# Fused linear attention and softplus FFN on one core: another order of the first x, conversions ahead of softplus in tile 0, joined weights side by side

## The chip, the cores and the metric

The kernel runs on one core of a Trainium2 chip. The metric is the time of one execution in device microseconds; a kernel's time is the median of its runs. The engines are named as in the profile: PE is TensorE (PEld its weight loads), DVE VectorE, ACT ScalarE, POOL GpSimd, SP the queue of SyncE that issues the DMAs.

## What is computed

Attention without a score matrix, and behind it a feed-forward layer whose activation is softplus. There are 8 batches, 8 heads, 576 tokens a batch and 64 elements a head, so 4608 tokens of 512 elements for the layer, whose inner width is 2048.

```python
q_s = np.exp(q - np.max(q, axis=-1, keepdims=True))
q_s = q_s / (np.sum(q_s, axis=-1, keepdims=True) + 1e-09)
k_s = np.exp(k - np.max(k, axis=2, keepdims=True))
k_s = k_s / (np.sum(k_s, axis=2, keepdims=True) + 1e-09)
kv = np.einsum('bhsd,bhse->bhde', k_s, v)
x = np.einsum('bhsd,bhde->bhse', q_s, kv)        # then (4608, 512)
h = x @ w_in                                     # (4608, 2048)
g = np.maximum(h, 0.0) + np.log1p(np.exp(-np.abs(h)))
return g @ w_out
```

## The kernel before

The tokens go in 9 tiles of 512, the inner width in 16 blocks `j` of 128. A step is one pair (tile, j). The loop over steps gives out, in this order: `up` (the product of x with a block of w_in, into one of the two PSUM banks `ph`), the share of the next tile's attention that stands in this step's slots, the end of the last step's softplus, this step's `softplus`, and `down` of two steps before (the product of g with a block of w_out, into four banks `po`). Each engine works through its instructions in the order in which the code gives them out; waits between engines follow from the data.

Tile 0 is computed in full float32: four matmuls for `up` and four for `down` (each shown as two records). Later tiles use three products of a high and a low part (float32r) in place of each. Weights arrive as int64 words `w` and are converted during tile 0: `top_w` (L119, ScalarE), `scale_w` (L114, ScalarE), `sign_w` (L124, VectorE, or GpSimd for the first three) and `join_w` (L135, VectorE) leave a float32 for each int64, in every other word. `split_w` (L142) makes the high part on ScalarE and the low part on VectorE; the list `SPLITS` has the steps in which the 16 blocks are split, and a block must be split before tile 1 comes to it.

`attend(t + 1)` spreads the attention of the next tile over the 16 steps of a tile. For the k and v of a pair of heads (a unit `h`) there are six parts: `top` (VectorE, the maximum over chunks, `mx`, L184, whose transposition L186 stands on TensorE at the end of the step), `across` (the maximum over the transposed tile, L200, and its transposition L201), `shift` (L205, subtraction on VectorE), `product` (the exponential L211 on ScalarE, and the k-v products L216 on TensorE at the end of the step), `scale` (L226, L227: r) and `split` (L240 `kv_hi` on ScalarE, L243 `kv_lo` on VectorE). Units h and h + 2 share a PSUM bank `att` and one of two buffers of k and v. When the products of unit h are given out, the DMA of the unit after next is issued (L169, the bulk, and L172, its tail). The slots of tile 1 and tile 2 are `2*h + i` for i in (0, 1, 2, 3, 4, 4). `q_unit` has 12 parts for the softmax of q, and `x_unit` makes x of q and kv (`q_lo`, L330, and the products L337 to L339).

Softplus (L387) has four ScalarE rows (L395 to L398) and three VectorE rows: L399 `(w - 1) - u`, L400 `max(ph, 0) - w`, which is the last reader of the PSUM bank `ph`, and L401. In tile 0 the conversions of w(j+2) are given out behind softplus(j).

The start, up to the first `up`, follows an order written by hand: a string of names, of which "u" are kv units, "q" the softmax of q, "x" the first x (transpose, product, copy for each pair of heads), and "t m s j" the conversions of the first weights.

## Time and profile before

| | |
|---|---|
| time, median of 3 runs | 921.27 us (919.81 to 922.92) |
| profiled execution | 920.85 us, span 919.1 us, granted clock 0.991 |
| PE busy | 883.2 us (96%) |
| DVE busy | 700.7 us (76%) |
| ACT busy | 582.7 us (63%) |
| POOL busy | 67.0 us (7%) |

The span is the time from the first to the last instruction of the profiled execution; 1.75 us of the execution lie outside it. Busy is the time in which an engine had an instruction under way. A row of the timeline has the start, the duration, the engine, the line, the operation, the tile written and those read, their shapes and, in brackets, how long the engine was idle before and which instruction ended that wait.

### The profile page before, as it was taken

To read this page: it belongs to the slowest core of one execution; us is meant where nothing else is said; L and a number is where in the kernel's file an instruction comes from. 1 tells how busy PE (TensorE), PEld (TensorE's weight loads), DVE (VectorE), ACT (ScalarE), POOL (GpSimd) and SP (SyncE) were. 2 spreads that over 40 slices of the span, in tenths; PEclk is the share of its full clock that TensorE was granted. 3 is DMA by queue.
4 is the path that set the end of the run, shared out by engine and by line. 5 is a ranking of instruction groups with operands and counts; after the bars stand their busy time and mean duration, and the time that the engine had idled before them with its cause. 6 is when DMAs were issued, how large, how long until landed. Compare 5 with 4: busy or idle time off the path is not lost.

```text
span 919.1 us, 11673 instructions
## 1 busy us (share of the span) xinstructions
PE 883.2 (96%) x4196; PEld 680.2 (74%) x4196; DVE 700.7 (76%) x1094; ACT 582.7 (63%) x982; POOL 67.0 (7%) x119
## 2 busy tenths in 40 slices
PE   3799989989999999999999999999999999999998
PEld 2343444667788888888888888888888888888886
DVE  8798878788778877887688768976897676765553
ACT  4666566767656665666576657665675566656554
POOL 2302300000000100020002000100110000000000
PEclk9899989999999999999999999999999999999999
DMA  9945101111013101301130113011200110001001
GB/s 313 381 141 195 52 0 47 46 53 32 21 46 98 36 17 47 98 23 30 46 98 9 44 46 98 1 52 46 84 16 1 46 47 1 1 1 47 0 1 46
DMA packets 49034, 55.28 MB, mean 60 GB/s; under 512 B 2256, under 2 KB 39120, under 8 KB 47824
## 3 DMA queue, kind: packets, MB, share of 16 engines
q1 hardware_dynamic: 48400, 54.27, 17.9%
q8 instruction: 33, 0.54, 0.2%
q10 hardware_dynamic: 576, 0.26, 0.1%
q14 instruction: 25, 0.20, 0.1%
HBM read 45.09 MB, written 9.44 MB: 59 GB/s over the span
## 4 chain that ended last, share of the span: by engine, by line
PE 83%; DVE 8%; ACT 5%; issue 2%; DMA 1%; POOL 0%; SPq 0%; DVEq 0%; ACTq 0%; POOLq 0%
PE ph L382 12%; PE po L427 12%; PE po L429 12%; PE po L428 12%; PE ph L383 12%; PE ph L384 12%; PE ph L377 3%; PE po L423 3%; PE att L216 2%; DVE w L138 1%; DVE w L128 1%; PE att L339 1%; PE att L338 1%; PE att L337 1%; DMA kvt<-in_kv_tail 1%
## 5 line engine op out<-in xcount | busy, mean ns | idle before, releaser
L429 PE MATMUL po<-w,g_lo 128*128 128x512 f32 x480 | 187.2, 390 | 1.9 <-DVE g_lo L407 1.9
L382 PE MATMUL ph<-x,w 128*128 128x512 f32 x480 | 188.8, 393 | 0.0
L427 PE MATMUL po<-w,g_hi 128*128 128x512 f32 x480 | 187.6, 391 | 0.0
L383 PE MATMUL ph<-x,w 128*128 128x512 f32 x480 | 186.9, 389 | 0.0
L428 PE MATMUL po<-w,g_hi 128*128 128x512 f32 x480 | 186.9, 389 | 0.0
L384 PE MATMUL ph<-x,w 128*128 128x512 f32 x480 | 186.8, 389 | 0.0
L399 DVE SCALAR_TENSOR_TENSOR w<-w,u 128x512 f32<-128x512 f32 x134 | 92.5, 690 | 117.1 <-ACT w L397 116.9
L406 ACT CAST g_hi<-l 128x512 fp32r<-128x512 f32 x128 | 79.5, 621 | 137.1 <-DVE l L401 134.9
L395 ACT ACTIVATE u<-ph 128x512 f32<-128x512 f32 x134 | 80.2, 598 | 55.6 <-PE ph L384 50.7
L401 DVE SCALAR_TENSOR_TENSOR l<-l,ln,w 128x512 f32<-128x512 f32 x128 | 96.3, 752 | 14.6
L429 PEld LDWEIGHTS po<-w,g_lo 128*128 128x128 f32 x480 | 90.1, 188 | 21.7 <-DVE g_lo L407 2.7
L382 PEld LDWEIGHTS ph<-x,w 128*128 128x128 f32 x480 | 90.4, 188 | 19.7 <-issue 0.6
L384 PEld LDWEIGHTS ph<-x,w 128*128 128x128 f32 x480 | 90.1, 188 | 19.0
L427 PEld LDWEIGHTS po<-w,g_hi 128*128 128x128 f32 x480 | 90.2, 188 | 18.0
L383 PEld LDWEIGHTS ph<-x,w 128*128 128x128 f32 x480 | 90.2, 188 | 17.9
L428 PEld LDWEIGHTS po<-w,g_hi 128*128 128x128 f32 x480 | 90.1, 188 | 17.8
L407 DVE TENSOR_TENSOR g_lo<-l,g_hi 128x512 fp32r<-128x512 f32 x128 | 87.1, 680 | 15.5 <-ACT g_hi L406 14.1
L400 DVE SCALAR_TENSOR_TENSOR w<-ph,w 128x512 f32<-128x512 f32 x134 | 92.6, 691 | 4.6
L397 ACT ACTIVATE w<-u 128x512 f32<-128x512 f32 x134 | 84.8, 633 | 4.2
L396 ACT ACTIVATE u<-u 128x512 f32<-128x512 f32 x134 | 84.7, 632 | 4.3
L398 ACT ACTIVATE l<-u 128x512 f32<-128x512 f32 x128 | 79.2, 619 | 12.5 <-DVE g_lo L407 12.5
L377 PE MATMUL ph<-x,w 128*128 128x512 f32 x128 | 61.6, 627 | 0.0
(136 smaller groups left out, 1020.7 us busy)
## 6 DMA issues: line engine op xcount, KB each, us to landing
kvt<-in_kv SPq DMA_DIRECT2D x30, 512.0 KB, 4.8
qt<-in_q SPq DMA_DIRECT2D x9, 1024.0 KB, 4.8
w<-in_w_in SPq DMA_DIRECT2D x16, 512.0 KB, 8.1
w<-in_w_out SPq DMA_DIRECT2D x16, 512.0 KB, 8.9
out<-w SPq DMA_DIRECT2D x32, 256.0 KB, 2.3
kvt<-in_kv_tail SPq DMA_DIRECT2D x28, 64.0 KB, 4.5
x<-in_kv SPq DMA_DIRECT2D x2, 512.0 KB, 9.4
out<-x SPq DMA_DIRECT2D x4, 256.0 KB, 2.4
```

The costliest lines, as they stand in the source:

```text
L377: nc.tensor.matmul(ph, lhsT=y[:, h * P:(h + 1) * P], rhs=x0[:, h], start=h == 0, stop=h == HP - 1)
L382: nc.tensor.matmul(ph, lhsT=w_hi, rhs=x_hi, start=h == 0, stop=False)
L383: nc.tensor.matmul(ph, lhsT=w_lo, rhs=x_hi, start=False, stop=False)
L384: nc.tensor.matmul(ph, lhsT=w_hi, rhs=x_lo, start=False, stop=h == HP - 1)
L397: nc.scalar.activation(w, u, AF.Copy, bias=1.0)
L399: nc.vector.scalar_tensor_tensor(out=w, in0=w, scalar=1.0, in1=u, op0=ALU.subtract, op1=ALU.subtract)
L400: nc.vector.scalar_tensor_tensor(out=w, in0=ph, scalar=0.0, in1=w, op0=ALU.max, op1=ALU.subtract)
L401: nc.vector.scalar_tensor_tensor(out=l, in0=l, scalar=ln1, in1=w, op0=ALU.subtract, op1=ALU.add)
L407: nc.vector.tensor_tensor(out=g_lo, in0=l, in1=g_hi.bitcast(F32), op=ALU.subtract)
L427: nc.tensor.matmul(po, lhsT=g_hi[:, ms], rhs=w_hi, start=j == 0, stop=False)
L428: nc.tensor.matmul(po, lhsT=g_hi[:, ms], rhs=w_lo, start=False, stop=False)
L429: nc.tensor.matmul(po, lhsT=g_lo[:, ms], rhs=w_hi, start=False, stop=j == NJ - 1)
```

## The change

The joined float32 weights now lie in the first half of their place, one next to the other (`whole_w`), and `up`, `down` and `split_w` of tile 0 read them there. The order of the start is another: `up` of step 0 is given out product by product (`up0` to `up3`), two of them between the first x products; the swap of q's sums goes by halves (`q12`, `q13`), both of q's divisions are on VectorE, and three of four x copies on ScalarE. In tile 0 the conversions of w(j+2) stand ahead of softplus(j), and the last two VectorE rows of softplus (`rest`) move behind the attention work of the next step. Eight blocks are split in tile 0 instead of six. For tiles 1 and 2 `top` of a kv unit stands directly behind the join, and `shift` goes to the step of `product`; tile 2's slots of q change by a step.

```diff
--- before.py
+++ after.py
@@ -37,7 +37,7 @@
 START = [P * sum(SUBS[:t]) for t in range(len(SUBS) + 1)]
 NTILE = len(SUBS)
 
-SPLITS = [10, 11, 12, 13, 14, 15, 16, 17, 18, 19, 20, 21, 22, 23, 24, 25]
+SPLITS = [6, 7, 8, 9, 10, 11, 12, 13, 16, 17, 18, 19, 21, 23, 25, 27]
 TOK = P * max(SUBS)
 assert START[-1] == NT
 
@@ -102,6 +102,9 @@
         w = raw[k].bitcast(dtype).rearrange("p z (n two) -> p (z n) two", two=2)
         return w[:, :, 0], w[:, :, 1]
 
+    def whole_w(k, dtype):
+        return raw[k].bitcast(dtype).rearrange("p z n -> p (z n)")[:, 0:2 * DM]
+
     def halves(k, dtype):
 
         w = raw[k].bitcast(dtype).rearrange("p z (n e) -> p (z n) e", e=4)
@@ -136,12 +139,12 @@
 
         low, high = words(k, U32)
         nc.vector.scalar_tensor_tensor(
-            out=low, in0=high, scalar=3, in1=low, op0=ALU.logical_shift_left, op1=ALU.bitwise_or
+            out=whole_w(k, U32), in0=high, scalar=3, in1=low, op0=ALU.logical_shift_left, op1=ALU.bitwise_or
         )
 
     def split_w(k):
 
-        y, _ = words(k, F32)
+        y = whole_w(k, F32)
         parts[k] = wp.tile([P, 2, 2, DM], F32R, name=f"w{k - 1}" if k else "spare")
         hi, lo = (parts[k][:, i].rearrange("p z n -> p (z n)") for i in range(2))
         nc.scalar.copy(hi, y)
@@ -281,9 +284,9 @@
 
         copy = nc.vector.tensor_copy if t else nc.scalar.copy
         if t:
-            slow = [nc.gpsimd if t == 1 else nc.vector] * 2
+            slow = [nc.gpsimd if t == 1 else nc.vector] * 4
         else:
-            slow = [nc.vector, nc.gpsimd]
+            slow = [nc.vector, nc.gpsimd, nc.vector, nc.vector]
 
         def join():
             nc.vector.tensor_tensor(out=m, in0=m, in1=swapped(m, copy), op=ALU.max)
@@ -297,18 +300,30 @@
         def total(g):
             nc.vector.tensor_reduce(out=s[:, g * n:(g + 1) * n], in_=half[g], op=ALU.add, axis=AX.X)
 
+        other = []
+
+        def swap(g):
+
+            if not other:
+                other.append(sm.tile([P, TOK // 8], F32, name="other"))
+            for a in range(4):
+                z = a ^ 1
+                copy(other[0][32 * a:32 * a + 32, g], s[32 * z:32 * z + 32, g])
+
         def invert():
-            o = swapped(s, copy)
+            if not other:
+                swap(slice(0, 2 * n))
+            o = other[0]
             nc.vector.scalar_tensor_tensor(out=s, in0=s, scalar=EPS, in1=o, op0=ALU.add, op1=ALU.add)
             nc.vector.reciprocal(s, s)
 
         def divide(g):
-            slow[g].tensor_tensor(out=half[g], in0=half[g], in1=spread(s, g), op=ALU.mult)
+            slow[2 + g].tensor_tensor(out=half[g], in0=half[g], in1=spread(s, g), op=ALU.mult)
 
         return [
             lambda: top(0), lambda: top(1), join, lambda: shift(0), lambda: shift(1),
             lambda: power(0), lambda: power(1), lambda: total(0), lambda: total(1), invert, lambda: divide(0), lambda: divide(1),
-        ]
+        ] + [lambda g=g: swap(slice(g * n, (g + 1) * n)) for g in range(2) if not t]
 
     def x_part(t, h):
 
@@ -361,7 +376,7 @@
             nc.tensor.matmul(bank, lhsT=whole[:, h], rhs=qT[:, h], start=True, stop=True)
 
         def take():
-            if h % 2 == 0:
+            if h < HP - 1:
                 nc.scalar.copy(x0[:, h], bank)
             else:
                 nc.vector.tensor_copy(x0[:, h], bank)
@@ -369,13 +384,22 @@
         return [flip, product, take]
 
 
+    begun = {}
+
+    def up_whole(j, h):
+
+        if h == 0:
+            begun[j] = ps_h.tile([P, TOK], F32, name="ph")
+        y = whole_w(j, F32)
+        nc.tensor.matmul(begun[j], lhsT=y[:, h * P:(h + 1) * P], rhs=x0[:, h], start=h == 0, stop=h == HP - 1)
+
     def up(t, j):
+        if t == 0:
+            if j not in begun:
+                for h in range(HP):
+                    up_whole(j, h)
+            return begun.pop(j)
         ph = ps_h.tile([P, TOK], F32, name="ph")
-        if t == 0:
-            y, _ = words(j, F32)
-            for h in range(HP):
-                nc.tensor.matmul(ph, lhsT=y[:, h * P:(h + 1) * P], rhs=x0[:, h], start=h == 0, stop=h == HP - 1)
-            return ph
         for h in range(HP):
             w_hi, w_lo = (parts[j][:, i, 0, h * P:(h + 1) * P] for i in range(2))
             x_hi, x_lo = (x_part(t, h)[:, i] for i in range(2))
@@ -388,7 +412,7 @@
 
         if t == 0:
 
-            u, w = (tp.tile([P, TOK], F32, name=("u", "w", "l")[(2 * j + i) % 3]) for i in range(2))
+            u, w = (tp.tile([P, TOK], F32, name=name) for name in ("u", ("w", "l")[j % 2]))
             l = gp.tile([P, TOK], F32, name=("g_hi", "g_lo")[j % 2])
         else:
             u, w, l = (tp.tile([P, TOK], F32, name=name) for name in ("u", "w", "l"))
@@ -397,9 +421,13 @@
         nc.scalar.activation(w, u, AF.Copy, bias=1.0)
         nc.scalar.activation(l, u, AF.Ln, bias=1.0)
         nc.vector.scalar_tensor_tensor(out=w, in0=w, scalar=1.0, in1=u, op0=ALU.subtract, op1=ALU.subtract)
-        nc.vector.scalar_tensor_tensor(out=w, in0=ph, scalar=0.0, in1=w, op0=ALU.max, op1=ALU.subtract)
-        nc.vector.scalar_tensor_tensor(out=l, in0=l, scalar=ln1, in1=w, op0=ALU.subtract, op1=ALU.add)
-        return l
+
+        def rest():
+            nc.vector.scalar_tensor_tensor(out=w, in0=ph, scalar=0.0, in1=w, op0=ALU.max, op1=ALU.subtract)
+            nc.vector.scalar_tensor_tensor(out=l, in0=l, scalar=ln1, in1=w, op0=ALU.subtract, op1=ALU.add)
+            return l
+
+        return rest
 
     def split_g(l):
         g_hi, g_lo = (gp.tile([P, TOK], F32R, name=name) for name in ("g_hi", "g_lo"))
@@ -416,7 +444,7 @@
             g_hi, g_lo = g
             w_hi, w_lo = (parts[j][:, i, 1] for i in range(2))
         else:
-            y, _ = words(j, F32)
+            y = whole_w(j, F32)
         for m, po in enumerate(acc[t]):
             ms = slice(m * P, (m + 1) * P)
             if t == 0:
@@ -489,13 +517,14 @@
 
         warm = ps_h.tile([P, TOK], F32, name="ph")
         todo["warm"] = lambda: [nc.tensor.matmul(warm[:, 0:P], lhsT=ident, rhs=ident, start=True, stop=True) for _ in range(8)]
+        todo.update({f"up{h}": lambda h=h: up_whole(0, h) for h in range(HP)})
         todo["kv"] = kv_prefetch
         todo["w"] = lambda: [load_w(k) for k in range(5, 10)]
         todo["q"] = lambda: q_load(1)
         for name in (
-            "q0 q1 u00 q2 q3 q4 q5 u10 u01 u11 u02 u12 q6 u03 u13 u20 u30 u21 u31 u22 u32 t0 m0 s0 u23 u33 warm q7 q8 q9 "
-            "kv kv w u04 u14 u05 u15 q10 q11 x00 x10 x01 x11 t1 m1 u24 u34 u25 u35 x20 x30 x21 x31 s1 j0 x02 x12 x22 x32 "
-            "t2 m2 s2 j1 q"
+            "q0 q1 u00 q2 q3 q4 q5 u10 u01 u11 u02 u12 q6 u03 u13 u20 u30 q7 u21 u31 t0 m0 s0 q8 q12 q13 u22 u32 u23 u33 "
+            "warm kv kv w q9 u04 u14 u05 u15 q10 t1 x00 x10 x01 x11 x02 m1 s1 x12 q11 j0 u24 u34 u25 u35 up0 up1 "
+            "x20 x30 x21 x31 x22 x32 up2 up3 j1 t2 m2 s2 q"
         ).split():
             todo[name]()
 
@@ -521,13 +550,19 @@
             if t < B:
                 for h in range(HP):
                     if t <= ON_PE:
-                        slots = [2 * h + i for i in (0, 1, 2, 3, 4, 4)]
+                        slots = [(first, 2 * h)] + [2 * h + i for i in (1, 3, 3, 4, 4)]
                     else:
 
                         g, z = 5 * (h // 2), h % 2
                         slots = [g + i for i in (z, z + 1, z + 1, 3, 4, 4)]
                     lazy(lambda h=h: kv_unit(t, h, banks[h % 2], after=kv_next), slots)
-            lazy(lambda: q_unit(t), (3, 4, 5, 5, 6, 7, 8, 7, 8, 9, 9, 10) if t == 1 else (2, 3, 3, 4, 5, 6, 6, 7, 8, 8, 9, 10))
+            if t == 1:
+                slots = 3, 4, 5, 5, 6, 7, 8, 7, 8, 9, 9, 10
+            elif t <= ON_PE:
+                slots = 1, 2, 3, 4, 5, 5, 6, 6, 7, 8, 9, 10
+            else:
+                slots = 2, 3, 3, 4, 5, 6, 6, 7, 8, 8, 9, 10
+            lazy(lambda: q_unit(t), slots)
             for h in range(HP):
                 a = h + 11
                 lazy(
@@ -560,13 +595,15 @@
                     for fn in steps[NJ]:
                         fn()
             if soft:
-                pending.append((soft[0], split_g(soft[1]) if soft[0][0] else soft[1]))
+                pending.append((soft[0], split_g(soft[1]) if soft[0][0] else soft[1]()))
                 soft = None
             if slot:
-                soft = slot, softplus(t, j, ph)
+
                 if t == 0 and 2 < j + 2 < NJ:
                     for fn in (top_w, scale_w, sign_w):
                         fn(j + 2)
+                l = softplus(t, j, ph)
+                soft = slot, l() if t else l
                 for fn in last[j]:
                     fn()
             while pending and order.index(pending[0][0]) <= n - 2:
```

VectorE's order in tile 0, step 4: before, from the sign step and the join of w(5) to the end of softplus(4) (L128 sign, L138 join, `kv_lo` and `mx` are the kv units 0 and 2).

```order
L128 TENSOR_SCALAR w_302<-w_302 128x1024
L138 SCALAR_TENSOR_TENSOR w_302<-w_302 128x1024
L226 TENSOR_SCALAR r<-att_105 128x1
L227 RECIPROCAL r<-r 128x1
L243 SCALAR_TENSOR_TENSOR kv_lo_101<-att_105,r,kv_hi_93 64x64 x2
L205 TENSOR_TENSOR kvt<-kvt,att_106 128x10x64
L184 TENSOR_REDUCE mx<-kvt 128x128
L280 TENSOR_REDUCE m<-qt 128x32
L252 TENSOR_TENSOR kv_lo_100<-spare,kv_hi_92 128x128
L399 SCALAR_TENSOR_TENSOR u<-u,l 128x512
L400 SCALAR_TENSOR_TENSOR u<-ph,u 128x512
L401 SCALAR_TENSOR_TENSOR g_hi<-g_hi,ln_109,u 128x512
```

The same place of the changed program: L131 is the sign step, L423 the first row of softplus(3), L141 the join, L187 `mx`, L246 `kv_lo`, L426 and L427 the deferred rows of softplus(3).

```order
L131 TENSOR_SCALAR w_304<-w_304 128x1024
L423 SCALAR_TENSOR_TENSOR l<-l,u 128x512
L141 SCALAR_TENSOR_TENSOR w_304<-w_304 128x1024
L187 TENSOR_REDUCE mx<-kvt 128x128
L229 TENSOR_SCALAR r<-att_105 128x1
L230 RECIPROCAL r<-r 128x1
L246 SCALAR_TENSOR_TENSOR kv_lo_101<-att_105,r,kv_hi_93 64x64 x2
L283 TENSOR_REDUCE m<-qt 128x32
L255 TENSOR_TENSOR kv_lo_100<-spare,kv_hi_92 128x128
L426 SCALAR_TENSOR_TENSOR l<-ph,l 128x512
L427 SCALAR_TENSOR_TENSOR g_lo<-g_lo,ln_109,l 128x512
```

The maximum `mx` stands ahead of r and `kv_lo` instead of behind them and `shift`, and the row that reads `ph` stands behind all of the attention work of the next step.

VectorE's order in tile 1, step 4, before: from the last row of softplus to `g_lo`.

```order
L401 SCALAR_TENSOR_TENSOR l<-l,ln_109,w 128x512
L226 TENSOR_SCALAR r<-att_105 128x1
L227 RECIPROCAL r<-r 128x1
L243 SCALAR_TENSOR_TENSOR kv_lo_97<-att_105,r,kv_hi_89 64x64 x2
L205 TENSOR_TENSOR kvt<-kvt,att_106 128x10x64
L184 TENSOR_REDUCE mx<-kvt 128x128
L292 TENSOR_TENSOR qt<-qt,m 128x1024
L148 TENSOR_TENSOR w_1188<-w_483,w_1188 128x1024
L407 TENSOR_TENSOR g_lo<-l,g_hi 128x512
```

The same place of the changed program.

```order
L427 SCALAR_TENSOR_TENSOR l<-l,ln_109,w 128x512
L187 TENSOR_REDUCE mx<-kvt 128x128
L229 TENSOR_SCALAR r<-att_105 128x1
L230 RECIPROCAL r<-r 128x1
L246 SCALAR_TENSOR_TENSOR kv_lo_97<-att_105,r,kv_hi_89 64x64 x2
L295 TENSOR_TENSOR qt<-qt,m 128x1024
L435 TENSOR_TENSOR g_lo<-l,g_hi 128x512
```

Here too `mx` comes before r and `kv_lo`; `shift` (L205) and the split of a block (L148) no longer stand in this step.

TensorE's order at the start, before: warm-up products, the four x products (L361), `up` of step 0 (L377), the transposition of tile 1's first `mx`, and `up` of step 1.

```order
L491 MATMUL ph<-ident 128x128 x8
L361 MATMUL po_179<-w_160,spare 128x512
L361 MATMUL po_180<-w_160,spare 128x512
L361 MATMUL po_181<-w_160,spare 128x512
L361 MATMUL po_182<-w_160,spare 128x512
L377 MATMUL ph<-x_161,w_142 128x512 x4
L186 MATMUL att_105<-ident,mx 128x128
L377 MATMUL ph<-x_161,w_145 128x512 x4
```

The same place of the changed program (L376 x products, L394 `up`).

```order
L519 MATMUL ph<-ident 128x128 x8
L376 MATMUL po_179<-w_160,spare 128x512
L376 MATMUL po_180<-w_160,spare 128x512
L394 MATMUL ph<-x_161,w_142 128x512 x2
L376 MATMUL po_181<-w_160,spare 128x512
L376 MATMUL po_182<-w_160,spare 128x512
L394 MATMUL ph<-x_161,w_142 128x512 x2
L189 MATMUL att_105<-ident,mx 128x128
L394 MATMUL ph<-x_161,w_145 128x512 x4
```

Two products of `up` now stand between the second and the third x product.

## Rows read from the trace of the kernel before

**Rows 1.** The page, the chain that ended last: shares of the span by engine

```profile
PE 83%; DVE 8%; ACT 5%; issue 2%; DMA 1%; POOL 0%; SPq 0%; DVEq 0%; ACTq 0%; POOLq 0%
```

**Rows 2.** Stages: start, end, length, busy us of PE, PEld, DVE, ACT, POOL, then PEclk

```profile
33.40:161.00 127.60, 119.23 (x354) 54.15 (x352) 107.18 (x141) 85.70 (x125) 16.79 (x17) 0.96 0.33 119
161.00:259.00 98.00, 92.19 (x460) 71.31 (x459) 80.82 (x126) 65.87 (x108) 1.94 (x12) 1.00 0.14 44
259.00:900.00 641.00, 641.00 (x3211) 532.18 (x3210) 478.38 (x755) 405.89 (x705) 37.76 (x74) 1.00 0.12 37
```

**Rows 3.** Timeline of TensorE around the first x and step 1 of tile 0

```profile
28.27 5.31 PE L361 MATMUL po<-w,spare 128*128 128x512 f32 x8 [2.90 <-DVE w L358]
33.41 3.60 PE L377 MATMUL ph<-x,w 128*128 128x512 f32 x8
...
42.68 0.32 PE L201 MATMUL att<-ident,m 128*128 128x128 f32 x1 [2.12 <-DVE m L200]
```

**Rows 4.** Timeline of TensorE around its two long waits in tile 0

```profile
82.51 0.33 PE L186 MATMUL att<-ident,mx 128*128 128x128 f32 x1 [2.09 <-DVE mx L184]
82.67 5.30 PE L377 MATMUL ph<-x,w 128*128 128x512 f32 x8
...
124.21 0.42 PE L337 MATMUL att<-q_hi,kv_hi 128*128 128x64 f32 x1 [2.57 <-DVE q_lo L330]
...
126.14 5.36 PE L377 MATMUL ph<-x,w 128*128 128x512 f32 x7
```

**Rows 5.** Waits of VectorE for softplus, 46 to 161 us

```profile
DVE u L399 <- ACT u L397: 2.8, 3, 1.5
```

**Rows 6.** VectorE operations by form, 46 to 161 us

```profile
L138 DVE SCALAR_TENSOR_TENSOR w<-w 128x1024 uint32<-128x1024 uint32 x13 | 18.9, 1457 | 0.4
L128 DVE TENSOR_SCALAR w<-w 128x1024 uint8<-128x1024 uint8 x13 | 17.2, 1326 | 2.0 <-ACT w L117 1.9
L148 DVE TENSOR_TENSOR w<-w,w 128x1024 fp32r<-128x1024 f32 x5 | 6.1, 1223 | 1.3 <-ACT w L147 1.3
```

**Rows 7.** Timeline of all engines at step 4 of tile 0

```profile
58.62 0.67 SPq L172 DMA_DIRECT2D kvt<-in_kv_tail  x1
...
59.70 1.23 DVE L138 SCALAR_TENSOR_TENSOR w<-w 128x1024 uint32<-128x1024 uint32 x1
...
60.84 0.15 DVE L226 TENSOR_SCALAR r<-att 128x1 f32<-128x1 f32 x1
...
61.47 3.77 PE L423 MATMUL po<-w,g_hi 128*128 128x512 f32 x8
...
61.95 0.58 DVE L243 SCALAR_TENSOR_TENSOR kv_lo<-att,r,kv_hi 64x64 fp32r<-64x64 f32 x2 [0.76 <-ACT kv_hi L240]
...
62.56 0.82 DVE L205 TENSOR_TENSOR kvt<-kvt,att 128x640 f32<-128x640 f32 x1
...
63.30 1.30 DVE L184 TENSOR_REDUCE mx<-kvt 128x128 f32<-128x640 f32 x1
...
64.52 1.21 DVE L280 TENSOR_REDUCE m<-qt 128x32 f32<-128x1024 f32 x1
...
66.56 0.69 DVE L400 SCALAR_TENSOR_TENSOR u<-ph,u 128x512 f32<-128x512 f32 x1
66.70 0.73 ACT L211 ACTIVATE kvt<-kvt 128x640 f32<-128x640 f32 x1
```

**Rows 8.** DMA view of tile kvt, 50 to 75 us, fastest, median, slowest landing

```profile
DMA to landing us min/median/max: 3.8/3.9/4.1
```

**Rows 9.** Timeline at step 4 of tile 1, and one wait of a later step

```profile
189.52 0.58 DVE L243 SCALAR_TENSOR_TENSOR kv_lo<-att,r,kv_hi 64x64 fp32r<-64x64 f32 x2 [0.76 <-ACT kv_hi L240]
...
191.39 1.32 DVE L184 TENSOR_REDUCE mx<-kvt 128x128 f32<-128x640 f32 x1 [0.43 <-DMA kvt<-in_kv_tail]
...
192.76 0.33 PE L186 MATMUL att<-ident,mx 128*128 128x128 f32 x1 [0.76 <-DVE mx L184]
...
224.09 0.50 PE L429 MATMUL po<-w,g_lo 128*128 128x512 f32 x1 [1.88 <-DVE g_lo L407]
```

## The prediction

> **What bounds the kernel now.** I read the chain of work that ended last, then the table of stages, then the waits one by one. The chain says where the end of the program is decided: 83% of it is TensorE, 8% VectorE and 5% ScalarE [rows 1]. So a microsecond counts only where TensorE stands still or runs slowly, and the table of stages says where that is [rows 2]. From 259 us to 900 us TensorE is busy for all of 641.00 us; nothing in the diff alters its instructions there, and the softplus and attention work of that stretch lies beside it. What the change can move lies before 259 us: the start (0 to 33.4 us), tile 0 in full float32 (33.4 to 161 us, TensorE 119.23 of 127.60 us busy, VectorE 107.18) and the first part of tile 1 (161 to 259 us, 92.19 of 98.00). In tile 0 TensorE is idle for 8.4 us only, and VectorE, which does the sign step and the join of the weights, has 20.4 us free. Neither has much room, so each wait of one is nearly a wait of both.
>
> The waits of TensorE there have names. At the start it waits 2.90 us for the transposed q ahead of the first x products, and 2.12 us in step 1 for the second maximum of k [rows 3]. In tile 0 it waits 2.09 us at 82.51 for a column maximum `mx` and 2.57 us at 124.21 for a `q_lo`. Behind both stands an `up` at half speed: 8 records in 5.30 us where the usual is 3.60, and 7 in 5.36 where 7/8 of 3.60 is 3.15 [rows 3, 4]. So each of these two places costs more than its wait: 2.09 + 1.70 = 3.8 us and 2.57 + 2.21 = 4.8 us. The granted clock of the stretch is 0.96 [rows 2].
>
> **The change, part by part.** The sum is made against the profiled execution, 920.85 us (span 919.1), which is 0.42 us under the median of 921.27.
>
> 1. The order of the first x. The first two `up` products of step 0 now stand between x products 1 and 2, q's division leaves GpSimd, and the swap of sums goes by halves on ScalarE. At best both waits go: 2.90 + 2.12 = -5.0 us. At worst they are only moved, 0: step 0 still needs the join `j0` and all of `s1`, and in step 0 the column maximum of tile 1's first unit now stands behind the join. I take -2.0, under half, because what TensorE waits for is VectorE work, and the start has as much of that as before.
>
> 2. Weights side by side. `down` of tile 0 streams the joined weights; it takes 3.77 us for 8 records where `up`, which streams the contiguous x0, takes 3.60 [rows 3, 7]. If the stride is the reason, 16 steps x 0.17 = -2.7 us at best; if VectorE sets the pace, 0. I take -1.0. The Trainium skill, SBUF — State Buffer (section on the ports, the note on cachelines), says that accesses which hit the same 16-byte line at least twice run at full bandwidth, so that a stride of two float32 words costs nothing; the trace shows 0.17 us a step that this rule doesn't explain, and by the rule the term would be 0 and the sum 1 us higher. The join and the split themselves read and write as many elements as before: 1.22 us for the split, and the join's 1457 ns (with its collisions) stay [rows 6].
>
> 3. Conversions ahead of softplus. ScalarE now does the two conversions of w(j+2) before softplus(j), and VectorE puts `sign` and `join` between the first row of softplus and its rest. What it takes away: VectorE's waits for ScalarE, of which the rows show 1.9 us ahead of `sign` and 2.8 us in three waits of the `u` form of softplus [rows 5, 6]. For TensorE that is worth at most what the late `q_lo` costs, 4.8 us, and at least 0. I take -3.0, nearer to the upper end, since `q_lo` is late there only because VectorE is.
>
> 4. The attention slots of tile 1 and 2, in tile 0. `top` of a kv unit moves from behind `kv_lo` and `shift` to right behind the join. But its k arrives by DMA. In step 4 the tail's DMA is issued at 58.62 and takes 3.8 us at least, so it lands at 62.4 [rows 7, 8]. The join ends at 60.93, so VectorE, which goes in order, would stand for 1.5 us there; before it did r, `kv_lo` and `shift` in that time. What is queued behind it: mx 1.30, to 63.7; r and `kv_lo`, 1.69 from 60.84 to 62.53 in the rows, to 65.4; q's maximum 1.21, to 66.6; and only then the row `max(ph,0)-w` (L400 before, L426 after; 0.69), to 67.3. That row frees the PSUM bank that the next `up` writes, and in the changed kernel it is deferred behind all of this. TensorE is through with `down` at 61.47 + 3.77 = 65.24. So it waits some 2.1 to 2.4 us (by 0.28 for the little split of `whole`): +2.2, between 0, if the DMA lands earlier, and +3.9 with an `up` at half speed behind it (1.70 more). In step 6 the same place already costs 2.09 us; there I put +0.2. The idle VectorE, twice 1.5 us, and the wait for the exponential of k, which now directly follows `shift` in the same step (0.82 + 0.73, [rows 7]), make VectorE late by up to 4.5 us in a stretch where it has little room: +2.0, between 0 and +4.5.
>
> 5. The splits. Eight instead of six stand in tile 0, from step 6 on: two more of 1.22 us and a wait of some 0.3 us each [rows 6] are 3.0 us of VectorE: +1.5, between 0 and +3.0.
>
> 6. Tile 1. There VectorE already waits 0.43 us for the tail's DMA ahead of mx, and TensorE 0.76 us for mx [rows 9]: the DMA is what ends last. After the change r and `kv_lo` come behind that mx. The next transposed maximum writes the bank that `kv_lo` reads, so it waits for another 1.69 us; two such units are +3.4. `shift` and exponential in one step put up to 1.55 us on the products of each unit; I take one of them, +1.5. The split beside the late `g_lo` goes away, and with it that wait of 1.88: -1.9 [rows 9]. Together +3.0, between -1.9 and +6.5.
>
> Sum: -2.0 - 1.0 - 3.0 + 2.2 + 0.2 + 2.0 + 1.5 + 3.0 = +2.9. From 920.85 this is 923.75, and with the 0.42 us to the median 924.2; I forecast 924.2 us. What can be told from no change here is about 0.3%, 2.8 us; the forecast lies 2.9 us above, at that edge.
>
> **The rivals.**
>
> Faster: VectorE gains its lead. If conversions ahead of softplus give VectorE enough lead that it reaches mx late, after the k has landed, its wait for the DMA is paid out of waits that go away anyway. Then the four named places in the start and tile 0 vanish: 5.0 + 3.8 + 4.8 = 13.6 us, less the two splits (3.0) and tile 1's 3.0: -7.6, about 914 us; with half of the places gone -1 to -3. For it: VectorE has 20.4 us free in tile 0, and a part of that is its waits for ScalarE. Against it: the landing is tied to the products of the step before (TensorE's work), not to VectorE, so a VectorE that is earlier only waits longer. It decides if mx shows no DMA wait in steps 4 and 6. Chance 0.27.
>
> No change: the start's gain (-2 to -5) and the attention slots' loss cancel; 919 to 923 us. Chance 0.23.
>
> Slower by the clock: each of the new waits of about 2 us (steps 4 and 6, and one or two in steps 8 to 10) is followed by an `up` at half speed, as the two were at 82.51 and 124.21. Three such steps more are 3 x 1.70 = 5.1 us: 929 us. Against it: the waits of tile 1 have no such step behind them; the granted clock is 1.00 in that stretch, against 0.96 in tile 0 [rows 2]. The Trainium skill, TensorE: Matmul & The Clock Gate (HAM oscillation), describes a kernel in which every wait for a DMA sends the array to half its clock; the two places here agree with it, the waits of tile 1 do not. Chance 0.14.
>
> My own case, slower by 1 to 7 us: 0.36.
>
> **How the numbers follow.** The likeliest case gives 924.2 us, with its own range of 921 to 928. The range for 8 in 10 reaches to the middle of the faster case and over the clock's: 912 to 931. Faster by over 0.3% has the faster case and a little of no change's lower end, 0.27; within 0.3%, no change and the lower part of my own case, 0.27; slower, the rest of my own case and the clock's, 0.46.
>
> **What would show it.** In the changed trace: the first x products without their 2.90 us; `down` of tile 0 at 3.60 us for 8 records (part 2); no wait of `sign` and of the first softplus row for ScalarE (part 3); a wait of mx for the k tail's DMA right behind the join in steps 4 and 6 of tile 0, and behind it TensorE waiting for the row `max(ph,0)-w` (part 4); in tile 1 the transposed maximum waiting for `kv_lo`, 1.5 us longer each (part 6). If tile 1's first `up` starts before 158 us instead of near 161, the faster rival is right. The prediction is wrong if the DMA lands before the join ends, or if TensorE's two slow `up`s disappear and none take their place.

## The result, and the profile after

The changed kernel takes 925.43 us (median of 8 runs, 922.78 to 927.95), the kernel before 921.53 us (8 runs). The ratio is 1.0038, with a 95% interval of 1.0025 to 1.005: slower by 3.5 us by the ratio, by 3.9 us by the medians. The profiled execution is the fastest of the 8 (922.78 us, span 921.0 us against 919.1), so its rows show some 2 us of the loss and not all of it.

The page of the changed kernel, busy times:

```profile
PE 879.6 (96%) x4196; PEld 678.8 (74%) x4196; DVE 699.3 (76%) x1094; ACT 582.2 (63%) x987; POOL 64.6 (7%) x118
```

TensorE is busy for less time than before (879.6 against 883.2 us) in a longer span. The table of stages, with the columns of [rows 2]:

```profile
33.40:161.00 127.60, 115.86 (x355) 53.20 (x355) 109.35 (x144) 86.78 (x127) 15.88 (x17) 0.97 0.33 119
161.00:259.00 98.00, 89.33 (x444) 69.48 (x443) 75.93 (x121) 60.72 (x103) 1.88 (x12) 0.98 0.12 37
259.00:900.00 641.00, 641.00 (x3210) 532.15 (x3209) 478.26 (x753) 406.99 (x708) 37.70 (x74) 1.00 0.12 38
```

From 33.4 to 161 us TensorE goes through as many records as before (355 against 354) in 3.4 us less busy time (115.86 against 119.23), most of which the faster `down` makes (16 steps of 0.17 us). From 161 to 259 us it does less work than before (444 records against 460, 89.33 us against 92.19), and the granted clock there is 0.98 instead of 1.00. From 259 us to 900 us nothing has changed. A fixed stretch holds other work in each kernel, though, so the timeline has to say where it went. TensorE's timeline of the start, to be read against [rows 3]:

```profile
26.71 1.88 PE L376 MATMUL po<-w,spare 128*128 128x512 f32 x4
...
35.89 0.33 PE L189 MATMUL att<-ident,mx 128*128 128x128 f32 x1 [1.22 <-DVE mx L187]
...
39.83 3.67 PE L394 MATMUL ph<-x,w 128*128 128x512 f32 x8
43.34 3.60 PE L451 MATMUL po<-w,g_hi 128*128 128x512 f32 x8
```

The x products come at 26.71 instead of 28.27 and at full speed (1.88 us for 4 records, where 8 took 5.31), `up` of step 1 at 36.06, behind a wait of 1.22 us for mx, and step 2's at 39.83, where before TensorE waited until 42.68 for a maximum. By `up` of step 3, 46.88, the changed kernel is 3.1 us ahead. `down` has 3.60 us for its 8 records, as `up`. Now step 4 of tile 0, the issue of the k tail, VectorE and then TensorE, the place of [rows 7]:

```profile
55.42 0.66 SPq L175 DMA_DIRECT2D kvt<-in_kv_tail  x1
55.50 1.22 DVE L141 SCALAR_TENSOR_TENSOR w<-w 128x1024 uint32<-128x1024 uint32 x1
59.45 1.28 DVE L187 TENSOR_REDUCE mx<-kvt 128x128 f32<-128x640 f32 x1 [2.73 <-DMA kvt<-in_kv_tail]
...
61.75 0.58 DVE L246 SCALAR_TENSOR_TENSOR kv_lo<-att,r,kv_hi 64x64 fp32r<-64x64 f32 x2 [0.76 <-ACT kv_hi L243]
...
63.79 0.69 DVE L426 SCALAR_TENSOR_TENSOR l<-ph,l 128x512 f32<-128x512 f32 x1
...
62.38 0.33 PE L189 MATMUL att<-ident,mx 128*128 128x128 f32 x1 [0.61 <-DVE kv_lo L246]
64.58 3.67 PE L394 MATMUL ph<-x,w 128*128 128x512 f32 x8 [1.87 <-ACT w L120]
```

VectorE ends the join at 56.72 and stands for 2.73 us in front of mx, until the k tail, issued at 55.42, has landed. r and `kv_lo` follow mx, and then q's maximum, a small split and the row L426 at 63.79 that frees the bank. TensorE waits 0.61 us for `kv_lo` and 1.87 us more ahead of `up`. The row names ScalarE's L120 as what ended that wait; but `up` starts at 64.58, 0.1 us after L426 ends at 64.48, and reads nothing that L120 makes: it is L426. The lead falls from 3.3 to 0.6 us here. The deferred row ends a wait ahead of `up` in steps 6, 8 and 10 too:

```profile
73.96 2.44 DVE L423 SCALAR_TENSOR_TENSOR l<-l,u 128x512 f32<-128x512 f32 x1
...
77.46 1.28 DVE L187 TENSOR_REDUCE mx<-kvt 128x128 f32<-128x640 f32 x1
...
82.86 5.37 PE L394 MATMUL ph<-x,w 128*128 128x512 f32 x8 [2.14 <-ACT w L120]
...
101.13 3.67 PE L394 MATMUL ph<-x,w 128*128 128x512 f32 x8 [1.61 <-ACT w L120]
...
119.48 5.37 PE L394 MATMUL ph<-x,w 128*128 128x512 f32 x8 [3.25 <-ACT w L120]
...
110.74 2.93 POOL L321 TENSOR_TENSOR qt<-qt,s 128x1024 f32<-128x1024 f32 x1
...
111.79 2.44 DVE L423 SCALAR_TENSOR_TENSOR l<-l,u 128x512 f32<-128x512 f32 x1
...
118.69 0.69 DVE L426 SCALAR_TENSOR_TENSOR l<-ph,l 128x512 f32<-128x512 f32 x1
```

In all four places `up` starts 0.10 us after L426 has ended. But there is no wait for the DMA in these three: in step 6 mx starts with none, and in steps 8 and 10 there is no mx. What stands ahead of the deferred row there is r and `kv_lo`, a split, in step 8 also a sum for q, and in steps 6 and 10 a row of softplus, L423, that takes 2.44 us instead of 0.69 (at 73.96 and 111.79) while GpSimd runs a `tensor_tensor` on q; before, such a collision hit other rows. Two of the waits have an `up` of 5.37 us behind them. Tile 1 nevertheless begins at 158.96 us, 2.0 us earlier than before (160.99). It loses all of that and as much again:

```profile
158.96 0.80 PE L406 MATMUL ph<-x,spare 128*128 128x512 f32 x1
...
188.80 1.31 DVE L187 TENSOR_REDUCE mx<-kvt 128x128 f32<-128x640 f32 x1 [2.42 <-DMA kvt<-in_kv_tail]
...
191.13 0.58 DVE L246 SCALAR_TENSOR_TENSOR kv_lo<-att,r,kv_hi 64x64 fp32r<-64x64 f32 x2 [0.76 <-ACT kv_hi L243]
...
191.76 0.33 PE L189 MATMUL att<-ident,mx 128*128 128x128 f32 x1 [2.13 <-DVE kv_lo L246]
...
193.13 0.63 PE L407 MATMUL ph<-x,w 128*128 128x512 f32 x1
...
207.71 0.33 PE L189 MATMUL att<-ident,mx 128*128 128x128 f32 x1 [2.07 <-DVE kv_lo L246]
...
214.55 0.80 PE L219 MATMUL att<-kvt 128*64 128x65 f32 x20 [1.05 <-issue]
```

In step 4 of tile 1 VectorE waits 2.42 us for the DMA, mx comes first, and the transposed maximum waits 2.13 us for `kv_lo` where it waited 0.76 for mx [rows 9]. Behind it the matmuls stand at 0.63 us for 0.39 for most of an `up` (they start 0.43 us apart instead of 0.23). The second such wait is 2.07, and the products of two units wait about 1.1 us each, one of them at 214.55.

### The profile page after: what moved, and what is told of

Read it like the earlier page. It is cut to its first block, busy times and chain, and to the rows that moved or that the text cites. A ratio compares the mean times of both kernels' runs of the same rounds, so it can differ in the third digit from the quotient of the medians.

```text
span 921.0 us, 11675 instructions
## 1 busy us (share of the span) xinstructions
PE 879.6 (96%) x4196; PEld 678.8 (74%) x4196; DVE 699.3 (76%) x1094; ACT 582.2 (63%) x987; POOL 64.6 (7%) x118
## 4 chain that ended last, share of the span: by engine, by line
PE 84%; DVE 6%; ACT 4%; DMA 3%; issue 2%; SPq 1%; POOL 0%; ACTq 0%; DVEq 0%
PE ph L406 12%; PE po L455 12%; PE po L457 12%; PE po L456 12%; PE ph L407 12%; PE ph L408 12%; PE ph L394 3%; PE po L451 3%; PE att L219 2%; DMA kvt<-in_kv_tail 1%; PE att L354 1%; PE att L353 1%; PE att L352 1%; DVE mx L187 1%; DVE w L131 1%
## 5 line engine op out<-in xcount | busy, mean ns | idle before, releaser
L423 DVE SCALAR_TENSOR_TENSOR w<-w,u 128x512 f32<-128x512 f32 x136 | 94.5, 695 | 114.9 <-ACT w L421 114.2
L419 ACT ACTIVATE u<-ph 128x512 f32<-128x512 f32 x144 | 86.0, 597 | 53.8 <-PE ph L408 49.8
L427 DVE SCALAR_TENSOR_TENSOR l<-l,ln,w 128x512 f32<-128x512 f32 x128 | 96.3, 752 | 15.0 <-DVE w L426 0.5
L426 DVE SCALAR_TENSOR_TENSOR w<-ph,w 128x512 f32<-128x512 f32 x136 | 94.0, 691 | 4.4
L420 ACT ACTIVATE u<-u 128x512 f32<-128x512 f32 x144 | 91.0, 632 | 4.6
L394 PE MATMUL ph<-x,w 128*128 128x512 f32 x128 | 62.1, 628 | 9.4 <-ACT w L120 8.9
```

Source lines behind the costliest of these rows:

```text
L394: nc.tensor.matmul(begun[j], lhsT=y[:, h * P:(h + 1) * P], rhs=x0[:, h], start=h == 0, stop=h == HP - 1)
L420: nc.scalar.activation(u, u, AF.Exp, scale=-1.0)
L423: nc.vector.scalar_tensor_tensor(out=w, in0=w, scalar=1.0, in1=u, op0=ALU.subtract, op1=ALU.subtract)
L426: nc.vector.scalar_tensor_tensor(out=w, in0=ph, scalar=0.0, in1=w, op0=ALU.max, op1=ALU.subtract)
L427: nc.vector.scalar_tensor_tensor(out=l, in0=l, scalar=ln1, in1=w, op0=ALU.subtract, op1=ALU.add)
```

## The experiments

All times are medians of five rounds against the kernel before on the same chip. Two variants are compared by their medians; by their ratios to the kernel before such a difference comes out up to 1.7 us larger or smaller. Where starts of tiles are compared, a tile is dated by the first `up` of tile 1 and of tile 2 in the profiled execution: 160.99 and 265.43 us before, 158.96 and 267.37 us in the changed kernel.

**The slots of the attention of tiles 1 and 2 as before**, the rest of the change kept.

```diff
-                        slots = [(first, 2 * h)] + [2 * h + i for i in (1, 3, 3, 4, 4)]
+                        slots = [2 * h + i for i in (0, 1, 2, 3, 4, 4)]
...
-                slots = 1, 2, 3, 4, 5, 5, 6, 6, 7, 8, 9, 10
+                slots = 2, 3, 3, 4, 5, 6, 6, 7, 8, 8, 9, 10
```

> The changed kernel with the attention slots of tiles 1 and 2 as before (top behind kv_lo and shift, shift a step ahead of product, q's slots of tile 2 too). Theory (mx, standing ahead of r and kv_lo and waiting for the k tail's DMA, is what costs): the two waits of the transposed maximum for kv_lo in tile 1 (2.13 and 2.07 us) shrink to those of before (0.76 and 1.71) and the half-speed up behind one of them goes, and in tile 0 the waits ahead of up at 64.58 and 82.86 (1.87 and 2.14 us) go; 916 to 919 us, 6 to 9 us under the changed kernel. Rival (the deferred rows of softplus and the two more splits cost, the slots don't): 923 to 926 us, and the waits ahead of up in steps 5, 7, 9 and 11 stay.

908.03 us, ratio 0.9859 (0.9845 to 0.9873) to the kernel before: 17.4 us under the changed kernel, about twice what the theory allowed. VectorE at step 4 of tile 1 in this kernel, and the starts of the two tiles:

```profile
180.78 0.58 DVE L246 SCALAR_TENSOR_TENSOR kv_lo<-att,r,kv_hi 64x64 fp32r<-64x64 f32 x2 [0.76 <-ACT kv_hi L243]
181.39 0.82 DVE L208 TENSOR_TENSOR kvt<-kvt,att 128x640 f32<-128x640 f32 x1
182.12 1.32 DVE L187 TENSOR_REDUCE mx<-kvt 128x128 f32<-128x640 f32 x1
```

```profile
152.43 0.80 PE L406 MATMUL ph<-x,spare 128*128 128x512 f32 x1
...
252.88 0.39 PE L406 MATMUL ph<-x,spare 128*128 128x512 f32 x1
```

r, `kv_lo` and `shift` fill the time until the k has landed, and mx follows with no wait. Of the gain, 6.5 us lie in tile 0 (152.43 against 158.96) and 8.0 in tile 1. Of the waits ahead of `up` in steps 5 and 7 of tile 0, 1.87 and 2.14 us, 0.94 and 0.97 are left, and one `up` of tile 0 still runs for 5.37 us. So the change has a part that is worth about 13 us and the slots take it away.

**Only `top` back behind `kv_lo`.**

```diff
-                        slots = [(first, 2 * h)] + [2 * h + i for i in (1, 3, 3, 4, 4)]
+                        slots = [2 * h + i for i in (0, 1, 3, 3, 4, 4)]
```

> The changed kernel with only top moved back behind r and kv_lo of the step; shift stays in the step of product. Theory (order of mx and kv_lo): the waits of the transposed maximum for kv_lo go, those of the k-v products (1.05 and 1.1 us in tile 1) stay; 918 to 921 us. Rival (shift and exponential in one step are the cost of the slots): within 1 us of the changed kernel, 924 to 926 us, with the products' waits unchanged.

916.95 us (0.9958, 0.9945 to 0.9971), 8.5 us under the changed kernel and 1 us under the theory's range; the rival is out. Tile 1 begins at 156.43, tile 2 at 260.84. TensorE's wait for the maximum, over the span:

```profile
PE att L189 <- DVE mx L187: 5.4, 4, 2.7
```

The transposed maximum no longer waits for `kv_lo` (5.7 us in the changed kernel, and 1.2 for mx), but 5.4 us for mx are left. The theory also had the waits of the k-v products stay; they are gone, so `shift` in the step of `product` makes them only where `top` stands first.

**Only `shift` back in the step ahead of `product`.**

```diff
-                        slots = [(first, 2 * h)] + [2 * h + i for i in (1, 3, 3, 4, 4)]
+                        slots = [(first, 2 * h)] + [2 * h + i for i in (1, 2, 3, 4, 4)]
```

> The changed kernel with shift of a kv unit back in the step ahead of product; top stays directly behind the join, q's slots stay. With top alone moved back the time was 916.95 us, with all slots back 908.03, so 9 us of the slots' 17 lie with shift and q's slots. Theory (both halves cost on their own, by VectorE's order ahead of kv_lo and by products that wait for shift and exponential): 915 to 919 us, without the products' waits of 1.05 and 1.1 us, with the transposed maximum still waiting some 2 us for kv_lo. Rival (top's place is the cost and shift only adds when top stands there): 922 to 926 us.

919.33 us (0.9971, 0.9956 to 0.9986), 6.1 us under the changed kernel and 0.3 above what the theory gave; the rival is out. The two halves give 8.5 and 6.1 us apart and 17.4 together with q's slots of tile 2, so they add up roughly; q's slots were not tried by themselves. Of the 6.1 us the profiled executions show 2.1 only (918.9 against 921.0 us), since this one is slower than its median and the changed kernel's faster. Waits of TensorE over the span and of VectorE in tile 0:

```profile
PE att L189 <- DVE kv_lo L246: 6.2, 4, 2.8
...
DVE mx L187 <- DMA kvt<-in_kv_tail: 8.8, 2, 5.1
```

The transposed maximum still waits for `kv_lo`, and VectorE stands in front of the k tail's DMA for up to 5.1 us at once. A VectorE that arrives earlier there only waits longer: in tile 0 mx starts 4.0 to 4.1 us after the tail's issue in all three such waits, at 59.45 in the changed kernel (issued at 55.42) and at 59.65 and 80.85 here (55.62 and 76.78). The waits of the k-v products are gone, as the theory said.

**The slots of the changed kernel in the kernel before**, nothing else (the whole `if t <= ON_PE` and q's slots from the diff).

```diff
-                        slots = [2 * h + i for i in (0, 1, 2, 3, 4, 4)]
+                        slots = [(first, 2 * h)] + [2 * h + i for i in (1, 3, 3, 4, 4)]
```

> The kernel before with the slots of the changed kernel alone. Theory (mx waits for the k tail's DMA whatever softplus does, and kv_lo behind it holds the transposed maximum in tile 1): slower by 5 to 10 us, 926 to 931 us, with the transposed maximum waiting some 2 us for kv_lo twice in tile 1. Rival (the slots cost only where the row that frees the PSUM bank is deferred behind them): 920 to 924 us.

939.1 us, ratio 1.0183 (1.0162 to 1.0205): 17 us slower, twice what was expected, and as much as the slots cost on top of the rest of the change. The rival, that they cost only where the row that frees the bank is deferred, is out. Waits of TensorE over the span, and the starts of tiles 1 and 2:

```profile
PE att L186 <- DVE kv_lo L243: 7.9, 4, 2.6
...
171.27 0.82 PE L382 MATMUL ph<-x,spare 128*128 128x512 f32 x1
...
282.91 0.39 PE L382 MATMUL ph<-x,spare 128*128 128x512 f32 x1
```

Tile 1 begins 10.3 us later than before and tile 2 17.5 us later. The four waits for `kv_lo` are 7.9 us, where before TensorE waited 4.6 us for mx; its waits for `q_lo` grow from 5.6 to 9.7 us, and the k-v products wait 5.3. In tile 0 VectorE stands for 0.4 us only in front of the DMA, so the DMA isn't what costs the 10.3 us there; its waits for ScalarE ahead of `sign` and of softplus' first row are 16.1 us of tile 0, before 9.3. Which of the new slots makes them was not taken apart. The collisions with GpSimd don't: the rows of VectorE that they lengthen take some 3.1 us too long in tile 0 here, 4.4 before (an estimate: each row's time less the shortest of its form). By the same estimate it is 5.7 us in the changed kernel and 3.8 with the slots as before, so up to 2 of the 6.5 us between these two can be collisions.

**Conversions ahead of softplus and deferred rows in the kernel before**, nothing else.

```diff
-            u, w = (tp.tile([P, TOK], F32, name=("u", "w", "l")[(2 * j + i) % 3]) for i in range(2))
+            u, w = (tp.tile([P, TOK], F32, name=name) for name in ("u", ("w", "l")[j % 2]))
...
-        nc.vector.scalar_tensor_tensor(out=w, in0=ph, scalar=0.0, in1=w, op0=ALU.max, op1=ALU.subtract)
-        nc.vector.scalar_tensor_tensor(out=l, in0=l, scalar=ln1, in1=w, op0=ALU.subtract, op1=ALU.add)
-        return l
+        def rest():
+            nc.vector.scalar_tensor_tensor(out=w, in0=ph, scalar=0.0, in1=w, op0=ALU.max, op1=ALU.subtract)
+            nc.vector.scalar_tensor_tensor(out=l, in0=l, scalar=ln1, in1=w, op0=ALU.subtract, op1=ALU.add)
+            return l
+        return rest
...
-                soft = slot, softplus(t, j, ph)
                 if t == 0 and 2 < j + 2 < NJ:
                     for fn in (top_w, scale_w, sign_w):
                         fn(j + 2)
+                l = softplus(t, j, ph)
+                soft = slot, l() if t else l
```

> The kernel before with the conversions ahead of softplus and the deferred rows alone. The changed kernel with the slots of before is 13 us faster than the kernel before. Theory (most of that is this part, since with the rows given out at once the time rose by 12 us): 911 to 915 us. Rival (it is the sum of many small things, start, side by side and splits): 917 to 921 us.

909.15 us, ratio 0.9862 (0.9841 to 0.9883): this part alone is worth 12 us, more than the theory gave it. The stage of tile 0 in its table of stages, VectorE's wait for the DMA there, and the first `up` of tile 1:

```profile
33.40:161.00 127.60, 125.31 (x390) 59.38 (x389) 108.63 (x150) 91.51 (x135) 13.32 (x17) 1.00 0.33 119
...
DVE mx L184 <- DMA kvt<-in_kv_tail: 2.3, 1, 2.3
...
149.72 0.82 PE L382 MATMUL ph<-x,spare 128*128 128x512 f32 x1
```

TensorE is busy for 125.31 of 127.60 us at a granted clock of 1.00, where before it was 119.23 at 0.96 (the last 11.3 us of the stretch are tile 1 here). Tile 1 begins 11.3 us earlier than before. VectorE still waits for the k tail, 2.29 us, but with `kv_lo` already done nothing of TensorE's hangs on that.

**The rows deferred, the conversions behind softplus**, in the kernel before: as above, with the three conversions behind `softplus`.

> The kernel before with the last two rows of softplus deferred in tile 0, but the conversions behind softplus as before. Theory (conversions ahead and deferral only gain together: the first row of softplus still waits for its three ScalarE rows, and the deferred row frees the PSUM bank later): 919 to 926 us. Rival (the deferral alone makes the gain of 12 us, since it lets VectorE do attention work first): 908 to 912 us.

922.4 us, ratio 1.0001 (0.9989 to 1.0014): the deferral alone gains nothing, as the theory said. Waits of VectorE in tile 0 and of TensorE over the span:

```profile
DVE w L128 <- ACT w L117: 10.0, 8, 1.9
...
PE ph L377 <- DVE l L402: 6.7, 6, 2.9
```

The sign step now waits 10.0 us for ScalarE's conversions, and TensorE 6.7 us ahead of `up` for the deferred row's bank.

**The conversions ahead, the rows not deferred**, in the changed kernel.

```diff
-                pending.append((soft[0], split_g(soft[1]) if soft[0][0] else soft[1]()))
+                pending.append((soft[0], split_g(soft[1]) if soft[0][0] else soft[1]))
...
-                soft = slot, l() if t else l
+                soft = slot, l()
```

> The changed kernel with the two deferred VectorE rows of softplus given out at once in tile 0, behind its first row; the conversions stay ahead of softplus on ScalarE. Theory (the row that frees the PSUM bank stands too late): the four waits ahead of up in tile 0 (1.87, 2.14, 1.61, 3.25 us, two with a half-speed up) shrink to under 1 us each, and VectorE waits 0.3 to 1 us a step more for ScalarE; 919 to 923 us. Rival (VectorE's total time, and not the place of that row, sets the pace of tile 0): 925 us or more, since the waits for ScalarE come on top.

937.29 us, ratio 1.0185 (1.0169 to 1.0202) to the kernel before, 12 us over the changed one. My theory is out, though its sign is there: of the four waits ahead of `up` 1.3 us are left. The deferred row frees the bank late, but given out at once it stands with VectorE behind four ScalarE rows that now come after the conversions, and TensorE waits elsewhere, in tile 0 6.1 us for `q_lo`, 7.0 ahead of k-v products and 3.5 for `kv_lo`. VectorE in tile 0:

```profile
DVE w L131 <- ACT w L120: 10.1, 11, 1.7
```

So neither half gained by itself: both orders with one half leave about 10 us of VectorE waiting for ScalarE's conversions, and with both together no wait of `sign` is left in tile 0. The conversions ahead without the deferral were tried in the changed kernel only, not in the kernel before.

**The list SPLITS as before**, in the changed kernel.

```diff
-SPLITS = [6, 7, 8, 9, 10, 11, 12, 13, 16, 17, 18, 19, 21, 23, 25, 27]
+SPLITS = [10, 11, 12, 13, 14, 15, 16, 17, 18, 19, 20, 21, 22, 23, 24, 25]
```

> The changed kernel with the list SPLITS as before: six splits in tile 0, from step 10 on. Theory (two more splits on a full VectorE cost 1.5 us, and the gain in tile 1 is the 1.88 us wait for g_lo): 924 to 927 us. Rival (the splits are what makes VectorE late in steps 6 to 11): the waits ahead of up at 101.13 and 119.48 (1.61 and 3.25 us) go and the time is 919 to 922 us.

924.24 us, ratio 1.0035 (1.0019 to 1.0052) to the kernel before; the changed kernel's is 1.0038, so no difference that can be told. The first `up` of tiles 1 and 2:

```profile
155.14 0.80 PE L406 MATMUL ph<-x,spare 128*128 128x512 f32 x1
...
267.70 0.39 PE L406 MATMUL ph<-x,spare 128*128 128x512 f32 x1
```

Tile 1 begins 3.8 us earlier than in the changed kernel, and tile 2 0.3 us later: what the early splits cost in tile 0 they give back in tile 1. The time lies in the theory's range by that, at more than twice its two terms (1.5 and 1.88 us); the rival is out.

**The slots and SPLITS as before**, the rest of the change kept (both edits above).

> The changed kernel with the slots and the list SPLITS of before, against the one with the slots alone (908.03 us). Theory (with the slots of before VectorE has room, so two more splits in tile 0 cost nothing and take the late g_lo out of tile 1): 909 to 911 us. Rival (they cost VectorE 3 us in tile 0): 905 to 907 us.

905.89 us, ratio 0.9827 (0.9807 to 0.9847): the fastest kernel here, 2.1 us under the one with the slots alone. The theory is out: with the slots as before the early splits cost 6.3 us in tile 0 (tile 1 begins at 146.13 instead of 152.43) and give back 4.0 in tile 1. The rival's range holds, though it had 3 of the 6.3 us. The wait for `g_lo`, and the starts of tiles 1 and 2:

```profile
PE po L457 <- DVE g_lo L435: 1.9, 1, 1.9
...
146.13 0.80 PE L406 MATMUL ph<-x,spare 128*128 128x512 f32 x1
...
250.56 0.39 PE L406 MATMUL ph<-x,spare 128*128 128x512 f32 x1
```

**The same with every split a step earlier.**

```diff
-SPLITS = [10, 11, 12, 13, 14, 15, 16, 17, 18, 19, 20, 21, 22, 23, 24, 25]
+SPLITS = [9, 10, 11, 12, 13, 14, 15, 16, 17, 18, 19, 20, 21, 22, 23, 24]
```

> The fastest kernel so far (start, weights side by side, conversions ahead and deferred rows of the changed kernel, slots and SPLITS of before, 905.89 us) with every split one step earlier, 9 to 24 in place of 10 to 25. Theory (the wait of 1.9 us for g_lo in tile 1 comes from the split in front of it, and VectorE has room for one more split in step 9): 903.5 to 904.5 us, without that wait. Rival (the split moved into tile 0 costs there what it gives back, as SPLITS from 6 on did, 2.1 us): 905.5 to 908 us.

907.37 us, ratio 0.9839 (0.9817 to 0.9862). The medians are 1.5 us apart, but on this chip the kernel before was slower too (922.53 against 921.16 us), and the intervals of the two ratios overlap: no difference that can be told. The gain of the theory isn't there, and TensorE's wait for `g_lo` has stayed:

```profile
PE po L457 <- DVE g_lo L435: 1.8, 1, 1.8
```

This list still splits in step 24, as do the ones with that wait, while the changed kernel's does not and has none. But the changed kernel with the list SPLITS as before splits in step 24 too and has no such wait, so that split alone doesn't make it; what does was not tried by itself.

**The new start alone**, in the kernel before (the string, q's division and swap, the x copies, `up_whole`, as in the diff).

> The kernel before with the new order of the start alone (first up between the x products, swap by halves, q's division off GpSimd, x copies on ScalarE). Theory (the start's 3 us, seen at up of step 3, 46.9 against 50.0 us, are its own and stay): 917.5 to 919.5 us. Rival (VectorE sets the pace of tile 0, so the lead is used up by step 6): 920 to 922 us.

921.72 us, ratio 0.9995 (0.998 to 1.0009): no difference that can be told. `up` of step 3, and TensorE's waits over the span:

```profile
49.70 3.60 PE L391 MATMUL ph<-x,w 128*128 128x512 f32 x8
...
PE att L349 <- DVE q_lo L342: 7.4, 5, 2.7
PE att L186 <- DVE mx L184: 7.2, 5, 2.1
```

At `up` of step 3 this kernel is 0.3 us ahead of the kernel before (50.01), not 3.1: the lead that the changed kernel has there isn't the start's own, as my theory had it. With the conversions and deferred rows alone it is 0.8 us there (49.25), so most of it comes only with the parts together. The waits for `q_lo` have grown from 5.6 us to 7.4 and those for mx from 4.6 to 7.2: what TensorE gains it waits for VectorE.

**The weights side by side alone**, in the kernel before (`whole_w` in `join_w`, `up`, `down` and `split_w`).

> The kernel before with the joined weights side by side alone. Theory (the stride costs TensorE 0.17 us a step of down, 2.7 us over 16 steps, and tile 0 is near to TensorE's bound): 918.5 to 920.5 us, with down of tile 0 at 3.60 us for 8 records. Rival (down gets faster, but VectorE sets the pace): 920.5 to 922 us, with the 2.7 us as more idle time of TensorE.

920.39 us, ratio 0.9994 (0.9979 to 1.0009): no difference that can be told either, and the time lies between the two forecasts. `down` of tile 0, and TensorE's wait for `q_lo` over the span:

```profile
95.47 3.60 PE L426 MATMUL po<-w,g_hi 128*128 128x512 f32 x8
...
PE att L340 <- DVE q_lo L333: 6.7, 4, 3.4
```

`down` takes 3.60 us for 8 records instead of 3.77, and TensorE waits 6.7 us for `q_lo` where it waited 5.6, and 5.4 for mx where it waited 4.6. With these two in, the fastest kernel is 3.3 us under the one that has only the conversions and deferred rows, so the two seem to count once VectorE no longer sets the pace; this was not taken apart further.

## Why the prediction was right, and where its sizes were off

The direction and the time came out as forecast (924.2 us, measured 925.43), and that it came so near is luck: two terms were far too small, one a gain and one a loss, and cancelled. By stages the sum holds roughly in the profiled executions: up to the start of tile 1 its parts come to -0.1 us, measured -2.0, and in tile 1 to +3.0, measured +4.0 (108.4 us against 104.4).

Part 1, the start (-2.0). The wait of 2.90 us ahead of the x products is gone, and in the changed kernel there is a lead of 3.1 us by step 3. But the start alone leads by 0.3 us there, and at the end nothing can be told from 0, its worst case.

Part 2, side by side (-1.0). The 0.17 us of a step is the stride's: with the weights contiguous `down` takes 3.60 us. That VectorE would set the pace was named; alone the part changes nothing that can be told (0, within some 2 us). The Trainium skill's rule that a stride of two float32 words is free (SBUF — State Buffer, the note on cachelines) doesn't describe TensorE's streaming of these weights here.

Part 3, the conversions (-3.0, at best -4.8). This term was mis-sized: it is worth -12 us. The bound failed because I took only the late `q_lo` as what this part could win. The waits for mx and the half-speed `up`s behind both came from the same late VectorE. I also read only one of three forms of the wait for softplus; in the view of [rows 5] stand two more:

```profile
DVE l L399 <- ACT l L397: 1.7, 3, 0.6
...
DVE w L399 <- ACT w L397: 0.6, 1, 0.6
```

With them it is 5.1 us and not 2.8, and with `sign` 7.0; with the conversions and deferred rows alone 3.1 are left and none of `sign`. Tile 0 went from 127.6 us (33.41 to 160.99) by 11.3, which is nearly all of the idle and slow time that it had (8.4 us idle and 3.9 at half speed). That is more than the waits of VectorE that went away; how the rest comes about was not taken apart.

Parts 4 and 6, the slots (+2.2, +0.2, +2.0 in tile 0 and +4.9 of the +3.0 in tile 1, together 9.3). The steps are those that the traces show: the DMA wait of mx right behind the join (2.73 us in step 4 where I had 1.5, since the join ends 4.2 us earlier than before and the tail is issued only 3.2 us earlier; none in step 6, where I had a second), `kv_lo` behind it, the late row that frees the bank, the transposed maximum waiting for `kv_lo`. But the term was mis-sized, too: it is 17 us, by two comparisons. Of it 10.3 us lie in tile 0 in the kernel before, 6.5 in the changed one, and 7 to 8 in tile 1; I priced steps 4 and 6 of tile 0 and let the rest fade, where the delay of VectorE lasts to the end of the tile. In the kernel before the DMA wait that I built on is 0.4 us of tile 0, and the slots cost 17 us even so. And some of the half-speed `up`s that I had given to the rival of the clock come with it: the changed kernel has two in tile 0, as before, and one more in tile 1, and with the slots of before one in all.

Part 5, the splits (+1.5, at most +3.0, and -1.9 in part 6). Both sizes were too small: 3.8 us in tile 0 with the slots of the change and 6.3 with those of before, and about 4 us back in tile 1, where I had counted the wait for `g_lo` alone. With the slots of the change they balance, with those of before they cost 2.1 us net.

The rival "faster" is out, but not by the sign that I gave it. Its sign was that mx shows no DMA wait; the kernels that gain 12 and 13 us show one in step 4, of 2.29 and 1.36 us. What they have instead is `kv_lo` ahead of mx: nothing of TensorE's hangs on the wait then in tile 0, and the rest of the change gives 13 us and more. The sentence against the rival, that an earlier VectorE only waits longer, is what the runs show too: with mx behind the join it is 2.73, 3.72 and 5.11 us in front of the same DMA, as the join ends earlier against the tail's issue.

Open: what q's slots of tile 2 alone cost, and whether a third buffer for k and v (so that the DMA is issued a unit earlier) would let the new slots stand; neither was tried. The 2.65 us between the profiled execution of the changed kernel and its median have no trace.

## What to carry to other kernels

Give an in-order engine the work whose data is already there, and put what waits for a DMA behind it: `top` behind `kv_lo` instead of ahead of it is worth 8.5 us here, and with `shift` and q's slots back 17. An edit that moves one engine's work off another's path may need its partner: the deferred rows gain nothing alone, the conversions ahead without them lose 12 us in the changed kernel, and both win 12 together, so test the parts apart and in pairs. When many small waits follow from one late engine, price the whole idle and slow time of the stage as the gain's bound, not only the wait that carries that engine's name.

## What was not expected of the hardware

A row of softplus of 0.69 us took 2.44 us, and another 1.68 instead of 0.75, while GpSimd ran `tensor_tensor` for 2.93 us on q; before, the same happened to the join (2.7 us instead of 1.2). And a wait of 2.13 us in tile 1, between stretches in which TensorE was fully busy, was followed by most of an `up` at half its speed (0.63 us for 0.39, starts 0.43 us apart for 0.23), with a granted clock of 0.81 from 191 to 200 us, while the wait of 2.07 us at 207.71 had a clock of 1.00 behind it (208 to 216 us).
